# GLU and long convolution on one core: a list schedule with other transfer constants and ranks, the first tile split over two DMA queues, one weight cast moved to VectorE

## The chip, the cores and the metric

The kernel runs on one core of one Trainium2 chip. The metric is the device time of one execution in microseconds (us); the median of three runs counts. TensorE (PE) multiplies; VectorE (DVE) and ScalarE (ACT) do element-wise work; GpSimd (POOL) and SyncE (SP) mostly issue transfers; PEld is TensorE's weight load, which lies beside its matmuls.

## What is computed

For tokens x of 2048 x 512 the kernel computes a gated mix of a state-space convolution and a bilinear GLU (cut to what matters, with x = A_u):

```python
g = sigmoid((x * gate_w).sum(-1, keepdims=True))
K = 2.0 * einsum("dn,dnl->dl", C, exp(A * dt * l)).real      # 512 channels, 128 states, 2048 taps
a = irfft(rfft(x, 4096) * rfft(K, 4096))[:2048] + x * D_skip  # a causal convolution per channel
b = ((x @ w_gate) * (x @ w_up)) @ w_down                      # 512 -> 1792 -> 512
out = g * a + (1 - g) * b
```

All inputs are float32.

## The kernel before

**The GLU.** The 1792 hidden channels are 14 tiles of 128, in four groups (0-2, 3-5, 6-9, 10-13); the tokens are four columns of 512, and the 512 model channels four tiles kt of 128. To keep float32 accuracy, each operand is split in a high and a low part: ACT casts the high part to the matmul's type, and DVE subtracts it from the original, which leaves the low part. A product is then three matmuls of 128 x 128 by 128 x 512 (high-low, low-high, high-high; the first ones of the kernel in the other order, so that those that need low parts come last). The names: `xs` holds both parts of a token tile, `whi` and `wlo` the gate and up weights, `pg` and `pu` the two PSUM banks of gate and up. From them ACT copies `h` out of `pg` (which also frees that bank), DVE multiplies it by `pu`, ACT casts `hh`, DVE makes `hl`, and these multiply the down weights `dhi`, `dlo` into the bank `y`. `product` (line 668), `hidden` (684) and `down` (711) hold these steps; `evacuate` (722) takes `y` out.

**The convolution.** DVE, ACT and POOL make tables of powers, `x` and `v` (`x_table`, line 1099, and `v_table`, 1123); from these TensorE makes the kernel's taps (`k_block`, 1164) and then transforms of 128 points (`k_first`, `m_product`, `m_inverse`, `m_last`), whose PSUM tiles are all called `k`. `u_part` (819) loads the tokens a second time and computes the scores of the gate: DVE's `y<-in,w3s` in the trace.

**What sets the order.** Every step is a task with an engine, an estimated duration, the tiles that it reads and writes, a rank and, for a transfer, a cost `dma`. `Work.plan` (355) is a list scheduler: it always takes the task that can start first by its own model (ties by rank), and the instructions are issued in that order on each engine by `InOrder` (line 124, which is therefore the line of nearly all instructions in the profile). The model of a transfer is: `SENT` us after its issue it enters one of two modelled queues, which share the rate by `WEIGHT`; it needs `dma` by `DMA_RATE`; and `LANDED` us later its readers may start. `FETCH` and `BEYOND` are terms for the loading of TensorE's instructions, `ROOM` says how much an ordinary task may delay an urgent one, and `EASE` is a table that gives tasks of a given engine, tiles and duration a slack in us, a rank or a later place. The schedule is fixed when the kernel is built; on the chip each engine goes through its list and waits on semaphores.

**The start.** `first_loads` (577) issues the first token tile (`xsrc(0)`, 256 KB, tile `y`) on SP and the first 256 columns of the first weights (128 KB, tile `ev`: a strip of gate and a strip of up columns) on ACT's queue, then the other kt by SP. `warm` runs six plain matmuls on a zeroed tile while these transfers are under way. `first_split` (626) makes `whi` and `wlo` of each kt, and `split` (541) the parts of `xs`. Ahead of its first cast ACT has an ACT_TABLE_LOAD, which the compiler inserts.

The functions touched:

Of the kernel before, what the change touches and what calls it, by code (L numbers as in the profile page):

```python
# [10 lines left out]
F32 = mybir.dt.float32  # L11
# [7 lines left out]
P = 128  # L19
# [185 lines left out]
class Work:  # L205
# [15 lines left out]
    BLOCK, FIRST, LEAD, FETCH = 256, 193, 64, 5.0  # L221
    TABLE = 1.3
    ROOM = {"dve": 0.6, "act": 0.4}
    BEYOND = 60
# [3 lines left out]
        "act:k/e:0.4": (3, 0, 0),  # L228
        "act:pb/x:0.31": (0.0, 0, -60),
# [4 lines left out]
        "dve:in/whi/wlo:0.69": (0.0, 1, 0),  # L234
        "dve:k/in:0.42": (3, 0, 0),
        "dve:k/ri:0.7": (0.0, 1, 0),
        "pe:kt/k/ri/e:2.13": (0.0, 0, -200),
        "pool:ts:0.95": (2, 0, 0),
# [4 lines left out]
    SENT = {"sp": 1.15, "act": 1.15, "pool": 1.98}  # L243
    LANDED = {"sp": 1.79, "act": 1.79, "pool": 1.5}
# [205 lines left out]
def gated_mix_kernel(  # L450
# [126 lines left out]
    def first_loads():  # L577
# [6 lines left out]
        wsrc = wts[0][:, : 2 * D].rearrange("p (k d) -> p k d", k=2)  # L584
# [41 lines left out]
    def first_split(kt):  # L626

        hi, lo, t, k = *ws[0], raws["w0"], ("k", kt)
        cut = lambda x: x.rearrange("p (c d) -> p c d", c=2)[:, :, P * kt : P * kt + P]
        src = lambda: t.t[:, :, P * kt : P * kt + P]  # L630
        add("act", 0.38, lambda: act.copy(cut(hi.t), src()), r=[(t, k)], w=[(hi, k)], rank=0)
# [16 lines left out]
    def tokens(gi, ci, kt):  # L648

        x = xs[kt] = new("glu", "xs", [P, 2, D], F32R, 5)  # L650
        if gi:
            add("sp", 0.42, lambda: sp.dma_start(x.t.bitcast(F32), xs_d[ci, kt]), r=[(m_xs, (ci, kt))], w=[x], dma=422, rank=0)
# [921 lines left out]
```

## Time and profile before

| | |
|---|---|
| three runs | 581.23, 581.37, 582.0; median 581.37 us |
| the profiled execution | 581.93 us, of which the span 580.1 |
| TensorE busy | 573.5 us, 99% |
| DVE, ACT, POOL busy | 510.9, 401.6, 113.5 us (88%, 69%, 20%) |
| chain of waits that ended last | PE 97%, a DMA 1%, ACT 1%, DVE 1% |
| data moved | 136.28 MB, 235 GB/s on average |

Busy shares alone say that TensorE is the bound. What is not TensorE's is found in three views: the waits of PE (how long it stood, and for whom), the windows (busy time of PE in stretches cut at its stalls), and the timeline around each stall. A row of the timeline has its start, its length, engine, line, operation with output and inputs, shape, and in brackets the idle time before it with what ended it.

### The profile page before, as it was taken

What the parts mean: (1) busy time and instruction counts of PE and PEld (TensorE: products, weight loads), DVE (VectorE), ACT (ScalarE), POOL (GpSimd) and SP (SyncE); (2) the same over time, 40 slices, a digit from 0 to 9 for tenths busy, and PEclk for the clock granted to TensorE, in tenths of its full rate; (3) what the DMA queues carried; (4) which work ended last, traced back from release to release, by engine and by line L of the source; (5) the groups of instructions that cost most, each with busy time, mean ns of one, the idle gap of its engine ahead of it and who ended that gap; (6) DMA issues with size and microseconds to landing.
All of it is one profiled execution on the core that took longest, in us unless ns stands there. A gap on an engine that the chain in (4) does not pass through costs nothing.

```text
span 580.1 us, 14843 instructions
## 1 busy us (share of the span) xinstructions
PE 573.5 (99%) x5998; PEld 433.8 (75%) x5998; DVE 510.9 (88%) x812; ACT 401.6 (69%) x891; POOL 113.5 (20%) x159
## 2 busy tenths in 40 slices
PE   9999999999999999999999999999999999999997
PEld 6777776888886877788677878876868786776775
DVE  6999999999998999999999999997999996347655
ACT  5459888898588589967896775799877544343351
POOL 0003222311111150321132401102333103111011
PEclk9999999999999999999999999999999999999999
DMA  8999959998655797998779757978989439798986
GB/s 284 403 354 358 395 216 354 269 231 232 140 173 128 281 228 173 261 216 273 201 226 250 188 135 238 213 198 206 292 147 292 72 134 289 246 293 222 291 166 128
DMA packets 71687, 136.28 MB, mean 235 GB/s; under 512 B 6852, under 2 KB 35780, under 8 KB 69188
## 3 DMA queue, kind: packets, MB, share of 16 engines
q1 hardware_dynamic: 47668, 87.10, 43.7%
q0 software_dynamic: 23392, 47.98, 39.6%
q8 instruction: 47, 0.77, 0.6%
q10 hardware_dynamic: 560, 0.26, 0.2%
q14 instruction: 20, 0.16, 0.1%
HBM read 80.27 MB, written 55.05 MB: 233 GB/s over the span
## 4 chain that ended last, share of the span: by engine, by line
PE 97%; DMA 1%; ACT 1%; DVE 1%; issue 0%; DVEq 0%; ACTq 0%
PE pg L124 27%; PE y L124 27%; PE pu L124 27%; PE k L124 16%; DMA y<-in_xT 1%; ACT h L124 0%; DVE y L124 0%; ACT acc L124 0%; ACT xs L124 0%; DVE hl L124 0%; DVE dlo L124 0%; DVE kt L124 0%; DVEq L1568 0%; ACT whi L124 0%; DVE h L124 0%
## 5 line engine op out<-in xcount | busy, mean ns | idle before, releaser
L124 PE MATMUL pg<-xs,whi 128*128 128x512 f32 x448 | 138.9, 391 | 0.4 <-ACT whi L124 0.4
L124 PE MATMUL pu<-xs,whi 128*128 128x512 f32 x448 | 138.2, 390 | 0.0
L124 PEld LDWEIGHTS pg<-xs,whi 128*128 128x128 f32 x448 | 84.3, 188 | 17.7 <-ACT whi L124 0.6
L124 PEld LDWEIGHTS pu<-xs,whi 128*128 128x128 f32 x448 | 84.1, 188 | 17.0
L124 PE MATMUL y<-dhi,hl 128*128 128x512 f32 x224 | 90.2, 403 | 0.7 <-DVE hl L124 0.6
L124 PE MATMUL pg<-xs,wlo 128*128 128x512 f32 x224 | 89.9, 401 | 0.8 <-ACT h L124 0.7
L124 PE MATMUL pu<-xs,wlo 128*128 128x512 f32 x224 | 89.3, 399 | 0.0
L124 PE MATMUL y<-dlo,hh 128*128 128x512 f32 x224 | 87.6, 391 | 0.0
L124 PE MATMUL y<-dhi,hh 128*128 128x512 f32 x224 | 87.1, 389 | 0.0
L124 POOL DMA_DIRECT2D out<-acc x44 | 38.5, 930 | 171.6 <-ACT acc L124 171.0
L124 ACT COPY ev<-k 128x512 f32<-128x512 f32 x112 | 59.3, 597 | 15.8 <-PE k L124 13.3
L124 ACT CAST hh<-h 128x512 fp32r<-128x512 f32 x56 | 34.7, 620 | 41.7 <-DVE h L124 41.3
L124 DVE TENSOR_TENSOR h<-pu,h 128x512 f32<-128x512 f32 x56 | 38.6, 689 | 26.3 <-PE pu L124 23.9
L124 ACT ACTIVATE acc<-y,ngate 128x512 f32<-128x512 f32 x62 | 42.0, 689 | 24.3 <-PE y L124 23.2
L124 PEld LDWEIGHTS pg<-xs,wlo 128*128 128x128 f32 x224 | 42.1, 188 | 21.5 <-issue 10.1
L124 PEld LDWEIGHTS y<-dhi,hl 128*128 128x128 f32 x224 | 42.0, 187 | 21.6 <-issue 8.3
L124 ACT COPY h<-pg 128x512 f32<-128x512 f32 x56 | 33.0, 590 | 32.4 <-PE pg L124 28.6
L124 PEld LDWEIGHTS pu<-xs,wlo 128*128 128x128 f32 x224 | 42.0, 188 | 16.7 <-issue 7.0
L124 PEld LDWEIGHTS y<-dhi,hh 128*128 128x128 f32 x224 | 42.1, 188 | 9.0
L124 PEld LDWEIGHTS y<-dlo,hh 128*128 128x128 f32 x224 | 42.1, 188 | 8.1 <-issue 0.3
L124 DVE TENSOR_TENSOR hl<-h,hh 128x512 fp32r<-128x512 f32 x56 | 38.4, 686 | 3.6 <-ACT hh L124 3.1
L124 DVE TENSOR_TENSOR v<-m,v 128x896 f32<-128x896 f32 x32 | 34.0, 1084 | 0.2
(130 smaller groups left out, 959.1 us busy)
## 6 DMA issues: line engine op xcount, KB each, us to landing
xs<-xs_d SPq DMA_DIRECT2D x36, 512.0 KB, 5.8
out<-acc POOLq DMA_DIRECT2D x44, 256.0 KB, 6.4
raw<-in_wts SPq DMA_DIRECT2D x33, 256.0 KB, 4.9
xs_d<-xs SPq DMA_DIRECT2D x16, 512.0 KB, 6.8
su_d<-ev POOLq DMA_DIRECT2D x32, 256.0 KB, 6.1
y_d<-ts SPq DMA_DIRECT2D x28, 256.0 KB, 6.1
in<-su_d POOLq DMA_DIRECT2D x12, 512.0 KB, 8.0
sk_d<-ev SPq DMA_DIRECT2D x6, 1024.0 KB, 3.9
```

Source lines behind the costliest of these rows:

```text
L124: got = getattr(self.engine, name)(*args, **kw)
```

## The change

It has five parts.

1. Constants of the planner: `WEIGHT` of the second queue 1.58 to 1.24, `FETCH` 5 to 4, `ROOM` of DVE 0.6 to 1.0, `BEYOND` 60 to 90, `SENT` and `LANDED` of all queues, the `dma` cost of some fifteen transfers, the slack of `k_block` 1 to 2, and a new `EASE` table. None of it adds or removes an instruction; it gives another order.
2. The first token tile is brought by two transfers of 64 rows each, one on SP's queue and one on ACT's, ahead of the weights' there.
3. The gate and up columns of weight tile 0 are laid out on the host so that each kt's 256 columns lie together; `first_loads`, `first_split` and `product` follow.
4. For kt = 0 the high part of the weights is made by DVE (`tensor_copy`) and not by ACT.
5. `product` gets the number f in place of the weights, to choose the base of its columns.

```diff
-    WEIGHT = 1.0, 1.58
+    WEIGHT = 1.0, 1.24
...
-    BLOCK, FIRST, LEAD, FETCH = 256, 193, 64, 5.0
+    BLOCK, FIRST, LEAD, FETCH = 256, 193, 64, 4.0
     TABLE = 1.3
-    ROOM = {"dve": 0.6, "act": 0.4}
-    BEYOND = 60
+    ROOM = {"dve": 1.0, "act": 0.4}
+    BEYOND = 90
...
-        "act:ts/xs:0.62": (0.0, 2, 0),
-        "dve:ev/y:0.6": (3, 0, 0),
+        "dve:ev/y:1.23": (0.0, 0, 200),
...
-    SENT = {"sp": 1.15, "act": 1.15, "pool": 1.98}
-    LANDED = {"sp": 1.79, "act": 1.79, "pool": 1.5}
+    SENT = {"sp": 1.35, "act": 1.35, "pool": 1.86}
+    LANDED = {"sp": 1.56, "act": 1.56, "pool": 1.62}
...
+        flat = w0.t.rearrange("p k d -> p (k d)")
         for kt in range(KT):
 
-            t, k, ks = xt[kt // 2], kt % 2, slice(P * kt, P * kt + P)
-            add("sp", 0.42, lambda t=t, k=k, kt=kt: sp.dma_start(t.t[:, k], xsrc(kt)), w=[(t, k)], dma=256, rank=-1)
+            t, k, ks = xt[kt // 2], kt % 2, slice(2 * P * kt, 2 * P * kt + 2 * P)
             e, q = ("sp", sp) if kt else ("act", act)
-            add(e, 0.42, lambda q=q, ks=ks: q.dma_start(w0.t[:, :, ks], wsrc[:, :, ks]), w=[(w0, ("k", kt))], dma=128, rank=-1)
+            cuts = (slice(0, P // 2), slice(P // 2, P)) if kt == 0 else (slice(0, P),)
+            for n, cut in enumerate(cuts):
+                ex, qx = ("act", act) if n else ("sp", sp)
+                add(
+                    ex, 0.42, lambda t=t, k=k, kt=kt, cut=cut, qx=qx: qx.dma_start(t.t[cut, k], xsrc(kt)[cut]),
+                    w=[(t, (k, n)) if len(cuts) > 1 else (t, k)], dma=256 // len(cuts), rank=-1,
+                )
+            add(e, 0.42, lambda q=q, ks=ks: q.dma_start(flat[:, ks], wts[0][:, ks]), w=[(w0, ("k", kt))], dma=128, rank=-1)
...
-        add("act", 0.38, lambda: act.copy(cut(hi.t), src()), r=[(t, k)], w=[(hi, k)], rank=0)
+        if kt:
+            add("act", 0.38, lambda: act.copy(cut(hi.t), src()), r=[(t, k)], w=[(hi, k)], rank=0)
+        else:
+            add("dve", 0.35, lambda: dve.tensor_copy(cut(hi.t), src()), r=[(t, k)], w=[(hi, k)], rank=0)
...
-        base = which * D + kt * P
+        base = which * D + kt * P if f else 2 * kt * P + which * P
...
-        add("pe", 2.05, kgen, r=[x, v], w=[pk], rank=0, hold=[kt], count=256, slack=1.0)
+        add("pe", 2.05, kgen, r=[x, v], w=[pk], rank=0, hold=[kt], count=256, slack=2.0)
...
+    wts[0, :, : 2 * D] = wts[0, :, : 2 * D].reshape(P, 2, KT, P).transpose(0, 2, 1, 3).reshape(P, 2 * D)
```

What that does to the engines' lists is shown at three places. A row is line, operation, output and inputs, and in brackets the semaphores that it waits for (DMAHW are those of transfers on SP's and ACT's queues; two transfers of different numbers are two waits).

**The start, on ACT.** Before, from its first transfer to its third cast:

```order
L124 DMA ev<-in_wts 128x2x128
L124 DMA small<-in_rows 128x4
L124 ACT_TABLE_LOAD
L124 CAST xs<-y 128x512 [waits DMAHW1_49]
L124 CAST whi<-ev 128x2x128 [waits DMAHW0_49]
L124 CAST xs<-y 128x512 [waits DMAHW2_49]
```

Now:

```order
L124 DMA y<-in_xT 64x512
L124 DMA ev<-in_wts 128x256
L124 DMA small<-in_rows 128x4
L124 ACT_TABLE_LOAD [waits DMAHW1_49]
L124 CAST xs<-y 128x512 [waits DMAHW0_49]
L124 CAST xs<-y 128x512 [waits DMAHW2_49]
L124 CAST whi<-ev 128x256 [waits DMAHW4_49]
```

A transfer of half the token tile (64 rows) has come first in the list; the cast of `whi` for kt = 0 has gone; the first cast reads a tile that two transfers write, and one of its two waits, DMAHW1, which is SP's half, stands at the table load's row.

**The start, on DVE.** Before, from its first subtraction:

```order
L124 TENSOR_TENSOR xs<-y,xs 128x512 [waits DMAHW1_49,Activation_49]
L124 TENSOR_TENSOR wlo<-ev,whi 128x2x128 [waits DMAHW0_49,Activation_49]
L124 TENSOR_TENSOR xs<-y,xs 128x512 [waits DMAHW2_49,Activation_49]
L124 TENSOR_TENSOR wlo<-ev,whi 128x2x128 [waits DMAHW4_49,Activation_49]
L124 TENSOR_SCALAR small<-small 128x4 [waits DMAHW3_49]
```

Now:

```order
L124 TENSOR_TENSOR xs<-y,xs 128x512 [waits DMAHW1_49,DMAHW0_49,Activation_49]
L124 CAST whi<-ev 128x256 [waits DMAHW3_49]
L124 TENSOR_TENSOR wlo<-ev,whi 128x256 [waits DVE_49]
L124 TENSOR_TENSOR xs<-y,xs 128x512 [waits DMAHW2_49,Activation_49]
L124 TENSOR_TENSOR wlo<-ev,whi 128x256 [waits DMAHW4_49,Activation_49]
L124 TENSOR_SCALAR small<-small 128x4 [waits DMAHW5_49]
```

A cast of the weights' 256 columns has come in behind the first subtraction, which waits for both halves.

**Some 25 us in, on DVE and PE** (`hl_358` and `hl_376` are the same tile in the two kernels, the low part of the third hidden tile; `y_323` and its like are scores). DVE before:

```order
L124 TENSOR_TENSOR h_313<-pu_309,h_313 128x512 [waits PE_49,Activation_49]
L124 SCALAR_TENSOR_TENSOR y_341,gate_83<-in_181,w3s_162 128x512
L124 TENSOR_TENSOR dlo_349<-kt_153,dhi_329 128x512 [waits DMAHW4_49,Activation_49]
L124 SCALAR_TENSOR_TENSOR y_354,gate_83<-in_181,w3s_162 128x512 [waits DVE_49]
L124 TENSOR_TENSOR hl_358<-h_313,hh_343 128x512 [waits Activation_49]
L124 SCALAR_TENSOR_TENSOR y_360,gate_83<-in_181,w3s_162 128x512 [waits DVE_49]
L124 TENSOR_TENSOR xs_336<-ts_237,xs_336 128x512 [waits DMAHW5_49]
```

DVE now:

```order
L124 TENSOR_TENSOR h_313<-pu_309,h_313 128x512 [waits PE_49,Activation_49]
L124 SCALAR_TENSOR_TENSOR y_346,gate_83<-in_182,w3s_167 128x512 [waits DVE_49]
L124 TENSOR_TENSOR xs_336<-ts_238,xs_336 128x512 [waits DMAHW6_49,Activation_49]
L124 SCALAR_TENSOR_TENSOR y_356,gate_83<-in_182,w3s_167 128x512 [waits DVE_49]
L124 TENSOR_TENSOR dlo_364<-kt_158,dhi_354 128x512 [waits DMAHW5_49,Activation_49]
L124 TENSOR_SCALAR ngate_84<-gate_83 128x4 [waits Activation_49]
L124 TENSOR_SCALAR gate_83<-gate_83 128x4 [waits DVE_49]
L124 TENSOR_TENSOR hl_376<-h_313,hh_348 128x512
```

The low part of a token tile of the next column, dlo and the two steps on the gates now stand ahead of `hl`. PE before, from the second pair of down products to the third:

```order
L124 MATMUL y_345<-dhi_275,hl_302 128x512
L124 MATMUL y_345<-dlo_283,hh_295 128x512
L124 MATMUL y_345<-dhi_275,hh_295 128x512
L124 MATMUL y_331<-dhi_329,hl_358 128x512 [waits DVE_49]
L124 MATMUL y_331<-dlo_349,hh_343 128x512 [waits Activation_49]
```

PE now:

```order
L124 MATMUL y_342<-dlo_315,hh_290 128x512
L124 MATMUL y_342<-dhi_304,hh_290 128x512
L124 MATMUL pg_358<-xs_336,wlo_148 128x512 [waits Activation_49]
L124 MATMUL pg_358<-xs_336,whi_144 128x512 [waits DVE_49]
L124 MATMUL pg_358<-xs_336,whi_144 128x512
L124 MATMUL pu_368<-xs_336,wlo_148 128x512
L124 MATMUL pu_368<-xs_336,whi_144 128x512 x2
L124 MATMUL y_330<-dhi_354,hl_376 128x512 [waits DVE_49,Activation_49]
```

Six matmuls of the next column's `pg` and `pu` now stand between.

**Some 420 us in, on ACT** (`ts` are output tiles of the convolution, mixed with the gate; `h_5475` and `h_5426` are the same copy of a `pg` in the two kernels, which frees its bank). Before, from the last mixes:

```order
L124 ACTIVATE ts_5276<-ts_5276,gate_83 128x128 x5
L124 CAST dhi_5433<-raw_5303 128x512 [waits DMAHW3_49]
L124 CAST hh_5439<-h_5322 128x512 [waits DVE_49]
L124 COPY x_5445<-pb_4184 128x64 [waits PE_49]
L124 CAST dhi_5447<-raw_5309 128x512 [waits DMAHW4_49]
L124 COPY kt_5455<-k_5324 128x8x2x16
L124 COPY v_752<-ri_5155 128x32x4
L124 COPY v_752<-ri_5155 128x32x7
L124 COPY v_752<-ri_5155 128x32x4
L124 COPY v_752<-ri_5155 128x32x7
L124 COPY h_5475<-pg_5423 128x512 [waits DVE_49,PE_49,Activation_49]
```

Now:

```order
L124 COPY v_881<-ri_5124 128x32x7
L124 COPY x_5399<-pb_4104 128x64
L124 COPY h_5426<-pg_5379 128x512 [waits DVE_49,PE_49]
L124 CAST dhi_5429<-raw_5280 128x512 [waits DMAHW3_49]
L124 COPY ts_5436<-k_5408 128x2x256 [waits DMAHW2_49,PE_49]
L124 CAST dhi_5443<-raw_5306 128x512 [waits DMAHW4_49]
L124 COPY ts_5447<-k_5418 128x2x256 [waits PE_49]
L124 ACTIVATE v_881<-v_881 128x32x16 [waits DVE_49,Activation_49]
L124 ACTIVATE sq_5456<-v_881 128x512 [waits Activation_49]
L124 CAST hh_5475<-h_5426 128x512 [waits DVE_49]
L124 ACTIVATE ts_5436<-ts_5436,gate_83 128x128 x2
L124 ACTIVATE ts_5436<-ts_5436,gate_83 128x128 [waits DVE_49]
```

Before, the copy of `h` stands behind all sixteen mixes, two casts and four copies; now behind the four copies and ahead of the casts and of the first eight mixes. On PE a transform's sixteen matmuls (`k` from `w4_t`) now stand between the last `pg` of that copy and its `pu`, where none stood.

More of the change, by code (lines that the diff above doesn't have):

```diff
@@ L218 @@
     OVERLAP = {"act": 0.09, "dve": 0.08}
-    BLOCK, FIRST, LEAD, FETCH = 256, 193, 64, 5.0
+    BLOCK, FIRST, LEAD, FETCH = 256, 193, 64, 4.0
     TABLE = 1.3
-    ROOM = {"dve": 0.6, "act": 0.4}
-    BEYOND = 60
+    ROOM = {"dve": 1.0, "act": 0.4}
+    BEYOND = 90
     BEHIND = 1.3
     EASE = {
-        "act:k/e:0.4": (3, 0, 0),
-        "act:pb/x:0.31": (0.0, 0, -60),
+        "act:k/e:0.6": (3, 0, 0),
+        "act:k/ev:0.6": (0.0, 2, 0),
+        "act:kt/dhi:0.62": (3, 0, 0),
         "act:raw/whi:0.62": (0.0, 0, -60),
         "act:t/rt:0.77": (0.0, 0, -200),
-        "act:ts/xs:0.62": (0.0, 2, 0),
-        "dve:ev/y:0.6": (3, 0, 0),
-        "dve:in/whi/wlo:0.69": (0.0, 1, 0),
+        "dve:ev/y:1.23": (0.0, 0, 200),
         "dve:k/in:0.42": (3, 0, 0),
-        "dve:k/ri:0.7": (0.0, 1, 0),
-        "pe:kt/k/ri/e:2.13": (0.0, 0, -200),
-        "pool:ts:0.95": (2, 0, 0),
+        "dve:x/ps/ri/su/di/m:1.09": (0.0, 0, 60),
         "sp:w3s/w2s/v:1.3": (0.0, 1, 0),
@@ L655, in tokens @@
         split(x, x, (0, 1), ("x", gi, ci, kt))
[L656 removed]
+        add("sp", 0.42, lambda: sp.dma_start(xs_d[ci, kt], x.t.bitcast(F32)), r=[x], w=[(m_xs, (ci, kt))], dma=443, rank=2, after=16.0 + kt if ci == 0 else 0.0)
     def ahead(ci):
@@ L666, in gated_mix_kernel, with product @@
     THREE = ((1, 0), (0, 1), (0, 0))
-    def product(pg, which, w, x, kt, after, first):
-        base = which * D + kt * P
+    def product(pg, f, which, x, kt, after, first):
+        w = ws[f]
+        base = which * D + kt * P if f else 2 * kt * P + which * P
         part = ("k", kt) if first else which
@@ L694, in hidden @@
         for which, kt in pairs:
-            product(pg[which], which, ws[f], x[kt], kt, after, not steps[1:] and f == 0)
+            product(pg[which], f, which, x[kt], kt, after, not steps[1:] and f == 0)
         h = new("glu", "h", [P, D])
@@ L735, in evacuate @@
         elif gi == 0:
-            add("sp", 0.42, lambda: sp.dma_start(ov[:, t, :], acc.t), r=[acc], w=[(m_out, t)], dma=134)
+            add("sp", 0.42, lambda: sp.dma_start(ov[:, t, :], acc.t), r=[acc], w=[(m_out, t)], dma=196)
         else:
@@ L739, in evacuate @@
                 "pool", 0.95, lambda: pool_q.dma_start(ov[:, t, :], acc.t, accum_op=ALU.add),
-                r=[acc, (m_out, t)], dma=431, rows=[t],
+                r=[acc, (m_out, t)], dma=442, rows=[t],
             )
@@ L821, in u_part @@
         rs = slice(4 * t, 4 * t + 4)
-        add("sp", 0.42, lambda: sp.dma_start(ut.t, uv[:, rs, :]), w=[ut], dma=929, after=6.0 + (U_STEP + 1.0) * t)
+        add("sp", 0.42, lambda: sp.dma_start(ut.t, uv[:, rs, :]), w=[ut], dma=840, after=6.0 + (U_STEP + 1.0) * t)
         def score_of(j):
@@ L880, in first @@
                     ),
[L881 removed]
+                    r=[st], w=[(m_su, (q, n0))], dma=234,
                 )
@@ L1236, in k_first @@
                     ),
-                    r=[st], w=[(m_sk, (q, m)) for m in range(n0, n0 + n, 8)], dma=41 * n,
+                    r=[st], w=[(m_sk, (q, m)) for m in range(n0, n0 + n, 8)], dma=50 * n,
                 )
@@ L1249, in gated_mix_kernel, with w_load @@
     m_w4 = work.memory()
-    def w_load(tag, shape, src, kb=327):
+    def w_load(tag, shape, src, kb=394):
         t = new("mid", tag, shape, bufs=2)
@@ L1274, in m_load @@
                 ),
-                r=[(m, (q, n0)) for n0 in range(0, 32, 8 if w else 4)], w=[(t, (T, w))], dma=655 if w else 585,
+                r=[(m, (q, n0)) for n0 in range(0, 32, 8 if w else 4)], w=[(t, (T, w))], dma=574 if w else 544,
             )
@@ L1458, in m_last @@
                 lambda rs=rs, flat=flat: pool_q.dma_start(ov[:, rs[0] : rs[-1] + 1, cs], flat(), accum_op=ALU.add),
-                r=[*parts, *((m_out, r) for r in rs)], dma=119 * len(rs), rows=rs,
+                r=[*parts, *((m_out, r) for r in rs)], dma=129 * len(rs), rows=rs,
             )
@@ L1544 @@
         "in_xT": host(u[rows.T.reshape(L)].T),
-        "in_wts": host(
-            np.concatenate(
-                [by_tile(i["B_w_gate"]), by_tile(i["B_w_up"]), i["B_w_down"].reshape(NF, P, D)], axis=2
-            )
-        ),
+        "in_wts": host(wts),
         "in_prm": host(
```

18 lines of the change are left out of this document (8 added, 10 removed).

## The prediction

> **What bounds the kernel now.** First the page: the span, the busy times, and the chain of work that ended last.
>
> ```profile
> span 580.1 us, 14843 instructions
> PE 573.5 (99%) x5998; PEld 433.8 (75%) x5998; DVE 510.9 (88%) x812; ACT 401.6 (69%) x891; POOL 113.5 (20%) x159
> PE 97%; DMA 1%; ACT 1%; DVE 1%; issue 0%; DVEq 0%; ACTq 0%
> ```
>
> TensorE is busy for 99% of the span. The order of both kernels holds the same matmuls and the same number of switches between the GLU and the convolution, so the change can only move what TensorE does not fill. The waits of PE name it, in total, times and longest:
>
> ```profile
> PE k L124 <- DVE acc L124: 1.1, 1, 1.1
> PE pg L124 <- ACT h L124: 0.7, 1, 0.7
> PE y L124 <- DVE hl L124: 0.6, 1, 0.6
> PE pg L124 <- ACT whi L124: 0.4, 1, 0.4
> ```
>
> And the windows of PE, cut at the stalls, show where (length, busy time and matmuls, granted clock, DMA share, GB/s):
>
> ```profile
> 0.00:5.62 5.62, 4.21 (x7) 1.00 0.64 177
> 25.33:26.27 0.94, 0.38 (x2) 1.00 1.02 405
> 26.27:100.00 73.73, 73.62 (x404) 1.00 0.93 340
> 100.00:420.00 320.00, 320.00 (x3723) 1.00 0.84 216
> 420.00:422.00 2.00, 1.33 (x6) 1.00 0.77 234
> 422.00:576.40 154.40, 154.27 (x1780) 1.00 0.80 207
> 576.40:580.10 3.70, 0.00 (x0) 0.99 0.64 196
> ```
>
> Three things can move: the 5.62 us before the first real matmul, two stalls (at 25.3 and 420.6), and 0.11 + 0.13 us in the long windows. The 3.70 us after the last matmul have the same order of work in both kernels and stay. So the most that stalls can give back is below 2 us, 0.3%; a measurement of this kernel can tell about 0.2%, 1.16 us, from no change. The start decides the sign.
>
> **The start, before.** The longest first piece of the chain of waits, then ACT, DVE and PE in time (start, length, what ended the idle time):
>
> ```profile
> 0.74 3.88 DMA y<-in_xT
> ```
>
> ```profile
> 1.75 1.28 ACT L124 ACT_TABLE_LOAD   x1 [1.75 <-issue]
> 4.64 0.62 ACT L124 CAST xs<-y 128x512 fp32r<-128x512 f32 x1 [1.60 <-DMA y<-in_xT]
> 5.17 0.40 ACT L124 CAST whi<-ev 128x256 fp32r<-128x256 f32 x1
> ```
>
> ```profile
> 0.84 0.17 DVE L124 MEMSET acc<- 128x128 f32 x1 [0.84 <-PEq L1563]
> ...
> 5.29 0.69 DVE L124 TENSOR_TENSOR xs<-y,xs 128x512 fp32r<-128x512 f32 x1 [4.13 <-ACT xs L124]
> 5.90 0.42 DVE L124 TENSOR_TENSOR wlo<-ev,whi 128x256 fp32r<-128x256 f32 x1
> ```
>
> ```profile
> 1.06 4.21 PE L124 MATMUL k<-acc 128*128 128x512 f32 x6 [1.06 <-DVE acc L124]
> 5.62 1.17 PE L124 MATMUL pg<-xs,whi 128*128 128x512 f32 x2 [0.35 <-ACT whi L124]
> 6.63 0.40 PE L124 MATMUL pg<-xs,wlo 128*128 128x512 f32 x1
> 6.86 0.62 PE L124 MATMUL pu<-xs,whi 128*128 128x512 f32 x2
> ```
>
> The first tile lands at 0.74 + 3.88 = 4.62. ACT casts its high part from 4.64, then the weights' from 5.17; DVE makes the low parts from 5.29 and 5.90; the first real matmul starts at 5.62, the third at 6.63, and from there they come every 0.23 us (6.86 - 6.63). The table load of 1.28 us, at 1.75, costs nothing: it lies in the shadow of the transfer, and ACT then sits idle for 1.60 us.
>
> **The first tile by two queues.** The cast now needs two landings, one per queue. An instruction row has the other wait: in the order of the changed kernel it is the table load, inserted ahead of the cast, that holds the wait for SP's half, while the cast itself keeps the wait for ACT's half. If the load waits in its row, its cover is gone: it starts when SP's half is in, and the cast 1.28 us after that. When does the half land? At latest when the whole tile did, 4.62. For the other end, the data flow in the DMA view of the first 8 us (40 slices of 0.2 us):
>
> ```profile
> GB/s 0 0 0 0 0 0 0 0 10 92 154 133 205 259 218 205 189 202 205 251 306 348 391 331 326 372 331 394 374 399 333 399 341 343 364 325 384 382 330 333
> y<-in_xT SPq DMA_DIRECT2D x4, 256.0 KB, 4.8
> ev<-in_wts ACTq DMA_DIRECT2D x1, 128.0 KB, 4.3
> ```
>
> Bytes move from 1.6 on, so at most 3.0 us of the tile's 3.88 are its own flow, and half of its bytes would save 1.5 at the very best (landing 3.1). But the nearest row, a 128 KB transfer on ACT's queue beside a 256 KB one on SP's, took 4.3 us from issue to landing, longer than the 3.88 of the 256 KB tile: a transfer of half the size is no faster there. I take 0.2 us earlier, 4.42.
>
> The Trainium skill, "DMA: Bandwidth & Descriptors", Rules for kernel authors, speaks against this part: two transfers to disjoint partition halves are not worth it, since both spread over the same 16 DMA engines and serialize. By it the second of the two halves would land at 4.62, and the sum below would be up to 0.2 us higher; the 4.3 us row agrees with it as far as it goes.
>
> So ACT's cast starts at 4.42 + 0.02 + 1.28 = 5.72, 1.08 later than 4.64. ACT's first weight transfer goes out one issue later than before; it is needed only two steps later, on DVE.
>
> **The weights' high part by VectorE.** On DVE it stands behind the low part of x: so after 5.72 come 0.65 (5.29 - 4.64, from ACT's start to DVE's), 0.61 (5.90 - 5.29, one DVE step), the copy itself, and 0.05 until PE (5.62 against the end of ACT's at 5.57). No row of before shows such a copy on DVE; it lies between a memset of 128 columns, 0.17, and the subtraction of the same 256 columns, 0.42, and I take 0.30, the middle, since ACT's copy of the tile took 0.40. The first matmul then starts at 5.72 + 0.65 + 0.61 + 0.30 + 0.05 = 7.33. The low part of the weights follows on DVE, until about 7.7. The third matmul of the kernel starts two steps after the first: 7.79 if they run at 0.23 us, 8.34 if they take the 1.01 us they took before (6.63 - 5.62). Against 6.63 that is +1.16 or +1.71. I take +1.45 for the start; DVE's and ACT's following pieces each take less than the six matmuls (1.38 us) that they feed, and all landed by then, so nothing more is lost behind it. The ends: +0.2 with the half at 3.1 and the copy at 0.17, +2.0 with the half at 4.62, the copy at 0.42 and the slow pace.
>
> The re-laid columns of the first weights change the shape of a transfer from two strips per row to one; PE reads the same 128 columns, at no cost on its side.
>
> **The stall at 25.3.** DVE's and PE's rows:
>
> ```profile
> 23.10 0.69 DVE L124 TENSOR_TENSOR h<-pu,h 128x512 f32<-128x512 f32 x1 [0.26 <-PE pu L124]
> 23.71 0.68 DVE L124 SCALAR_TENSOR_TENSOR y<-in,w3s 128x512 f32<-128x512 f32 x1
> ...
> 24.32 0.69 DVE L124 TENSOR_TENSOR dlo<-kt,dhi 128x512 fp32r<-128x512 f32 x1
> ...
> 25.53 0.69 DVE L124 TENSOR_TENSOR hl<-h,hh 128x512 fp32r<-128x512 f32 x1
> ```
>
> ```profile
> 25.33 0.39 PE L124 MATMUL y<-dhi,hh 128*128 128x512 f32 x1
> 26.27 0.50 PE L124 MATMUL y<-dhi,hl 128*128 128x512 f32 x1 [0.56 <-DVE hl L124]
> ```
>
> From start to start PE lost 0.94 - 0.23 = 0.71 us because hl came 2.43 us behind h on DVE, behind a score, dlo and a score. In the new order 18 matmuls stand between the last pu and that y, where 12 stood, which gives hl 6 x 0.23 = 1.38 us more; but on DVE four steps of 0.61 (a score, the low part of x, a score, dlo) stand between h and hl where three stood, and two small ones on the gates, which I take at 0.15 each, near the 0.17 of the memset; so hl ends about 0.9 us later. 0.71 - 1.38 + 0.9 = 0.2 us stay; with 0.4 for the upper end I take -0.3 here.
>
> **The stall at 420.6.** ACT's and PE's rows:
>
> ```profile
> 419.77 1.46 ACT L124 COPY v<-ri 128x128 f32<-128x128 f32 x4
> 421.04 0.62 ACT L124 COPY h<-pg 128x512 f32<-128x512 f32 x1
> ```
>
> ```profile
> 420.42 0.61 PE L124 MATMUL pu<-xs,whi 128*128 128x512 f32 x2
> 421.71 0.50 PE L124 MATMUL pg<-xs,wlo 128*128 128x512 f32 x1 [0.67 <-ACT h L124]
> ```
>
> PE's second matmul started near 420.65, the next at 421.71: 1.06 - 0.23 = 0.83 us lost, since the copy that frees the bank stood behind sixteen mixes, two casts and four copies. In the new order that copy stands ahead of mixes and casts, and on PE a transform's sixteen matmuls come between this pg and its pu, so this stall goes. The next copy of h now stands behind eight mixes, one of which waits for DVE; if that copy is late, some comes back. I take -0.7 (from 0 to -0.83).
>
> **New stalls.** Most of the 812 and 891 instructions of DVE and ACT stand in a new order, with other due times for transfers. What that costs no trace shows; the order of before, made by the same planner, left two stalls of 0.7 to 0.8, so zero to two such ones bound it, and I take +0.3, the middle being high for an order fitted to landings.
>
> **Sum.** +1.45 - 0.3 - 0.7 + 0.3 = +0.75 us. The profiled execution took 581.93 (580.1 of span and 1.83 around it), which gives 582.7; it lies 0.56 above the median of the three runs, 581.37, so the forecast of the median is 582.1, slower by 0.13%. Ends: start +0.2 and both stalls gone, -1.2; start +2.0, two new stalls and none gone, +3.5.
>
> **Rivals.**
>
> *The clock is lost at the start (slower).* The rows of the warming matmuls and of others with the same 512 columns:
>
> ```profile
> L124 PE MATMUL k<-in,w_t 64*32 64x512 f32 x96 | 5.8, 595 | 0.0
> L124 PE MATMUL k<-acc 128*128 128x512 f32 x4 | 3.8, 1101 | 1.1 <-DVE acc L124 1.1
> ```
>
> The granted clock reads 1.00 throughout, yet the first took 1101 ns and not 595: half speed until about 6.6. Before, PE's idle time between the warming and the real work was 0.35 us; after, it would be 7.33 - 5.27 = 2.06. If the full speed has to be earned again from there, matmuls run at 0.23 x 1101/595 = 0.42; eight of them lose 1.5 us, and the time is 583.6. It decides if the third real matmul and those behind it still stand 0.4 apart. For it: in this trace the speed came only after the gap. Against it: full speed may come sooner than the warming ends in most executions. 18%.
>
> The Trainium skill, "TensorE: Matmul & The Clock Gate", Part 1, has this as a free-running window of about 3.4 us that must be busy before the clock goes to full; by it the loss depends on where the window falls in an execution. Only the two groups above bear on that here.
>
> *The load is not held (no change).* If the table load runs at 1.75 as before, since ACT runs it ahead of its wait, the cast starts at 4.44, the first matmul at 6.05, the third at 6.5 to 7.1: start +0.15, sum -0.55, 580.8. For it: nothing but that the load needs no data. Against it: an engine's row waits where it stands. 17%, two thirds of it within 0.2%.
>
> *The new order clears PE's way (faster).* Both stalls go whole (-1.54), no new one comes, and the two halves land near 3.1 (start +0.2): -1.34, 580.0. Its place is the two stalls; it decides when the start costs under 0.4 us. 8%.
>
> *New stalls (slower).* Two of 0.8 us at new places and the rest as in the forecast: start +1.45, stalls +1.6 - 1.0: +2.05, 583.4. 7%.
>
> **How the numbers follow.** The forecast has 50%, from 581.0 to 583.4, between the start's two paces and the stalls' bounds; a third of it lies above 582.53, where slower than 0.2% begins (17%), the rest within 0.2% (33%). With the clock (18%) and new stalls (7%), slower is 42%. Within 0.2%: 33 + 11 = 44%. Faster: 8 + 6 = 14%. The range leaves out half of the faster cases and the worst tail of the slow ones: 580.5 to 584.2.
>
> **What would show it.** Right: the table load starting at 4.3 to 4.7 and ending just ahead of the first cast; whi on DVE behind the low part of x; the first pg near 7.3; no wait of PE at 420 and a small one near 27. Wrong: the table load at 1.7; the first pg before 6.3; matmuls 0.4 apart up to 10 us; a wait of over 0.5 us elsewhere.

## The result: 1% slower, and the profile after

The changed kernel takes 587.89 us, median of four runs (587.79 to 589.28), against 581.68 for the kernel before in the same comparison: a ratio of 1.0099, interval 1.0077 to 1.0121. The forecast, 582.1 in 580.5 to 584.2, was too low by 5.8 us. The profiled execution of the changed kernel took 587.79, 5.86 more than that of before, and its parts can be set beside the prediction's.

From the page, the engines' busy time and the chain that ended last:

```profile
PE 575.4 (98%) x5998; PEld 435.0 (74%) x5998; DVE 511.7 (87%) x813; ACT 399.2 (68%) x890; POOL 113.6 (19%) x159
PE 86%; DMA 5%; issue 4%; POOL 1%; ACT 1%; DVE 1%; SPq 0%; DVEq 0%; POOLq 0%; ACTq 0%
```

TensorE still has the same 5998 instructions, but the chain now leaves it: DMA 5%, issue 4% and POOL 1%, which were 1%, 0% and nothing. ("Issue" is time in which an engine waits for nothing that the profile shows.) The waits of PE say where:

```profile
PE pg L124 <- DVE whi L124: 3.1, 1, 3.1
PE k L124 <- issue: 1.5, 2, 0.8
PE k L124 <- DVE acc L124: 1.1, 1, 1.1
PE y L124 <- DVE hl L124: 0.6, 1, 0.6
PE k L124 <- DMA in<-sk_d: 0.4, 1, 0.4
PE pg L124 <- ACT h L124: 0.2, 1, 0.2
```

**The start.** ACT, DVE and PE in time:

```profile
4.92 1.28 ACT L124 ACT_TABLE_LOAD   x1 [4.92 <-DMA y<-in_xT]
6.21 1.14 ACT L124 CAST xs<-y 128x512 fp32r<-128x512 f32 x2
```

```profile
6.87 0.69 DVE L124 TENSOR_TENSOR xs<-y,xs 128x512 fp32r<-128x512 f32 x1 [5.71 <-ACT xs L124]
7.48 0.28 DVE L124 CAST whi<-ev 128x256 fp32r<-128x256 f32 x1
```

```profile
1.06 3.76 PE L124 MATMUL k<-acc 128*128 128x512 f32 x6 [1.06 <-DVE acc L124]
7.91 1.19 PE L124 MATMUL pg<-xs,whi 128*128 128x512 f32 x2 [3.09 <-DVE whi L124]
8.89 0.63 PE L124 MATMUL pg<-xs,wlo 128*128 128x512 f32 x1
9.32 1.05 PE L124 MATMUL pu<-xs,whi 128*128 128x512 f32 x2
...
15.11 0.50 PE L124 MATMUL pg<-xs,wlo 128*128 128x512 f32 x1
```

The table load, which ran at 1.75 before, starts at 4.92 with the landing of the first tile's half, and the first cast right behind it. The first real matmul comes at 7.91 (5.62 before), the third at 8.89 (6.63). And they then run slowly: from 8.89 to 9.32 is 0.43, where it was 0.23. The windows of PE show the clock with it (length, busy time and matmuls, granted clock):

```profile
7.91:10.82 2.91, 2.91 (x7) 0.50 0.98 383
10.82:15.11 4.29, 4.29 (x18) 0.97 0.95 338
```

For these 2.9 us TensorE had half its clock. The matmul that opens the second hidden tile is the row at 15.11 above; before, it stood at 11.81, in the row below. So 3.30 us are lost by then, 2.29 until the first matmul and 1.0 behind it, where the clock is low.

```profile
11.81 0.50 PE L124 MATMUL pg<-xs,wlo 128*128 128x512 f32 x1
```

**The rest.** From there to the last matmul before had 564.2 us and the changed kernel 566.9, 2.7 more. PE's rows near 131, 418, 334 and 466; the last fence is the kernel before:

```profile
129.86 1.98 PE L124 MATMUL k<-v,x 128*32 128x64 f32 x124
132.53 0.31 PE L124 MATMUL k<-v,x 128*32 128x64 f32 x4 [0.69 <-issue]
...
416.20 1.88 PE L124 MATMUL k<-v,x 128*32 128x64 f32 x119
418.86 0.35 PE L124 MATMUL k<-v,x 128*32 128x64 f32 x9 [0.79 <-issue]
```

```profile
334.26 1.60 PE L124 MATMUL k<-in,w2s 32*32 32x512 f32 x32 [0.39 <-DMA in<-sk_d]
...
465.76 2.13 PE L124 MATMUL k<-in,w2s 32*32 32x512 f32 x32
```

```profile
457.94 1.99 PE L124 MATMUL k<-v,x 128*32 128x64 f32 x128
...
462.13 1.14 PE L124 MATMUL k<-in,w2s 32*32 32x512 f32 x32
```

The long runs of 128 small matmuls that make the kernel's taps break off for 0.69 and 0.79 us, 4 and 9 matmuls ahead of their end, and the profile shows nothing that they wait for; such a run went through before. In the window from 129 to 133 the DMA view has a transfer of the queue called instruction:

```profile
q8 instruction: 1, 0.02, 1.5%
```

so code that came late fits. But that queue brings 47 packets in the whole run, one in 12 us, and one of them in such a window says little: the cause is not shown. The pass at 466 took 2.13 us for 32 matmuls, and such a pass took 1.14 before; this profile doesn't say why, but in e6 and e17 below the same pass is broken by a wait for `kt` from DVE. The pass at 334 first waits for a transfer, the 0.4 of `in<-sk_d` above, and then takes 1.60. The stall at 420.6 is gone as forecast; the one at 25 stands at 31 now and costs 0.78 where it cost 0.71; one of 0.33 from start to start is new near 341. Start to start, the two breaks cost 1.8 (0.69 + 0.79 of it idle time), the pass at 466 1.0, the wait at 334 with its pass 0.9, the stall at 341 0.3 and the one at 31 0.1 more, less 0.83 for the stall that went: 3.3. The measured 2.7 is 0.6 less, which no single row shows.

### The profile page after: what moved, and what is told of

It is laid out like the page before. It is cut to its first block, busy times and chain, and to the rows that moved or that the text cites. A ratio compares the mean times of both kernels' runs of the same rounds, so it can differ in the third digit from the quotient of the medians.

```text
span 586.0 us, 14853 instructions
## 1 busy us (share of the span) xinstructions
PE 575.4 (98%) x5998; PEld 435.0 (74%) x5998; DVE 511.7 (87%) x813; ACT 399.2 (68%) x890; POOL 113.6 (19%) x159
## 4 chain that ended last, share of the span: by engine, by line
PE 86%; DMA 5%; issue 4%; POOL 1%; ACT 1%; DVE 1%; SPq 0%; DVEq 0%; POOLq 0%; ACTq 0%
PE y L124 24%; PE pg L124 23%; PE pu L124 23%; PE k L124 15%; DMA ts<-in_xT 1%; DMA kt<-in_wts 1%; DMA out<-acc 1%; POOL in L124 1%; DMA y<-in_xT 1%; DMA sk_d<-ev 1%; ACT ev L124 1%; POOL out L124 1%; SPq L124 0%; DVE y L124 0%; ACT h L124 0%
## 5 line engine op out<-in xcount | busy, mean ns | idle before, releaser
L124 PEld LDWEIGHTS k<-v,x 128*32 128x32 f32 x2048 | 29.5, 110 | 7.4 <-issue 6.4
```

What stands on the lines that cost most here:

```text
L124: got = getattr(self.engine, name)(*args, **kw)
```

## The experiments

Times are ratios to the kernel before in the same comparison, with their intervals; single rows are from each kernel's profiled execution. For the profiled executions two numbers are given: the start of the matmul that opens the second hidden tile (11.81 before, 15.11 changed), which is the start's cost, and the time from it to the start of the last matmul (564.2 and 566.9), the rest's.

### The start: what it costs, and why

`e12_after_again` is the changed kernel once more, without an edit.

> The changed kernel once more, beside the others on one chip. All theories: 0.8 to 1.2% slower than before; first real matmul near 7.9, matmuls 0.43 apart to about 10.5, two waits for issue near 131 and 418.

1.0092 (1.0073 to 1.0111): the loss is there again. Opening matmul 16.71, rest 566.3; of the two breaks only the one near 131 came (0.65).

`e1_early_table` gives ACT an operation that needs no transfer, so that the table load has somewhere else to go:

```diff
...
+        def small_in():
+            act.dma_start(small[:, 0], rows[1].rearrange("(p c) -> p c", c=KT))
+            act.copy(early, half_pi)
...
```

> The changed kernel with one ACT copy of 128x1 behind ACT's third transfer, so that the table load no longer stands behind the first tile's landing. Theory (load held by the first landing, and the long gap of PE costs its clock): load near 2.5, first cast at 4.9, first real matmul near 6.6 instead of 7.9, 1.3 us less, and up to 1.4 more if PE's clock is then full sooner: 585.2 to 586.6 beside 587.9. Rival (the halves' late landing or DVE's cast sets the start): first real matmul stays past 7.5, time within 0.5 us of 587.9.

```profile
2.45 1.28 ACT L124 ACT_TABLE_LOAD   x1 [2.45 <-issue]
3.74 0.19 ACT L124 COPY early<-fixed 128x1 f32<-128x1 f32 x1
4.40 0.62 ACT L124 CAST xs<-y 128x512 fp32r<-128x512 f32 x1 [0.47 <-DMA y<-in_xT]
```

ACT's rows: the load is back in the shadow, the cast at 4.40, the first real matmul at 6.10 (7.91). 1.0054 (1.0038 to 1.007): some 0.4% of the 0.95% come back, more than the 1.28 us of the load. The two breaks grew, to 1.5 and 1.7 from start to start.

`e17_act_cast` leaves the load where the change put it and gives the first weights' cast back to ACT:

```diff
-        if kt:
+        if True:
             add("act", 0.38, lambda: act.copy(cut(hi.t), src()), r=[(t, k)], w=[(hi, k)], rank=0)
```

> The changed kernel with the first weights' cast back on ACT, and the table load left behind the first landing; PE's list unchanged. Theory (load and cast each cost, and the later the start, the longer the slow clock): load at 4.9, first cast at 6.2, first real matmul near 7.2 instead of 7.9, 0.7 to 1.5 us less than the changed kernel: 0.65 to 0.85% above before. Rival (the load alone costs): first real matmul earlier but the time unchanged, 0.92 to 0.99%.

The first matmul came at 7.01 and the opening one at 14.41, 0.7 earlier, yet the time stayed: 1.0093 (1.0063 to 1.0122). The rival's number, but not its reason: the profile lost 1.0 at the pass near 332 (0.56 of it a wait for `in<-sk_d`), 1.13 for h near 340 and 1.5 at the pass near 465 instead (start to start), and shows no break of the long runs. `e11_early_act` has both repairs, with PE's list untouched.

> The changed kernel with the early ACT copy, and the first weights' cast back on ACT; PE's list unchanged. Theory: load out of the way, first cast near 4.4, cast of the weights at 4.95, first real matmul near 5.4 to 5.7 where it was 6.1 with DVE's cast: 0.3 to 0.7 us less at the start, clock full sooner; the code waits take part of it back: 0.3 to 0.5% above before. Rival (DVE's cast costs nothing, since the low parts bind): first real matmul earlier but the third one not, the same time as with the early copy alone, 0.55% above before.

1.0029 (1.0015 to 1.0044): together they bring back two thirds of the loss. In the profile the first matmul is at 6.09, the opening one at 12.80, and the rest is 564.4, that of before. So only 2.3 us of the 4.7 between the two profiles lie at the start: the rest was healed too, which no theory had said. The waits near 334 and 341 are gone in it, and so is the break near 130; a break of 0.7 near 413 and the late pass (1.99 us at 461) stay.

`e4_one_tile` brings the first tile by one transfer again:

```diff
-            cuts = (slice(0, P // 2), slice(P // 2, P)) if kt == 0 else (slice(0, P),)
+            cuts = (slice(0, P // 2), slice(P // 2, P)) if kt < 0 else (slice(0, P),)
```

> The changed kernel with the first tile by one transfer on SP's queue; the same list of PE. Theory (the second landing puts the load behind the first): load at 1.75, first cast near 4.65, first real matmul near 6.3, 1.6 us less, and 0.7 to 1.4 more by the clock: 584.9 to 586.3. Rival (the weights' cast on DVE is the start's cost): first real matmul later than 7, less than 0.9 us gained: 587.0 to 587.9.

The load ran at 1.66, the cast at 4.68, and the first matmul at 5.35, earlier than expected, since the weights' cast stood ahead of x on DVE here (4.88 and 5.33). But 1.0071 (1.0046 to 1.0096). In the profiled execution, the slowest of the six (589.74), the rest took 571.0, with breaks of 1.8 and 2.0 from start to start in the runs at 129 and 417, 0.8 at the pass near 332 and 1.1 for h near 340; a wait of 1.2 for h lies ahead of it.

`e14_start_in_place` puts the changed start into the kernel before, inside its tasks, so that PE keeps the order of before. (The first cast on DVE lies ahead of the low part of x there.)

```diff
...
+            def tile_in(t=t, k=k, kt=kt, cuts=cuts):
+                for n, cut in enumerate(cuts):
+                    (act if n else sp).dma_start(t.t[cut, k], xsrc(kt)[cut])
...
```

> The kernel before with its order kept on PE, and the changed start put into it: the first tile's halves on two queues, the weights re-laid, their first cast on DVE (here ahead of the low part of x). Theory (load behind the landing, then slow clock): load at 4.9, first cast at 6.2, first real matmul near 6.9, up to 1.4 us of slow matmuls, no wait for issue: 1.3 to 3 us, 0.2 to 0.5% above before. Rival (the loss is the new order's): within 0.2% of before.

1.0016 (1.0000 to 1.0033). Load at 4.90, first cast 6.19, first matmul 6.86, slow matmuls behind it (0.43 apart past 10 us), opening matmul 14.81, rest 564.7. The profiled execution, 585.49, was the slowest of its ten runs, which begin at 582.98. Its mean granted clock was 0.995 and that of the nine others 1.000, so what the clock takes varies by execution.

`e15_halves_in_place` does the same with the early copy and all casts on ACT.

> The kernel before with its order kept, the first tile's halves on two queues, the early ACT copy, all casts on ACT. Theory: load out of the way, first cast at 4.4 to 4.9 where it was 4.64, first real matmul 5.3 to 5.8: within 0.2% of before; the halves are worth 0.3 us at most. Rival (halves land earlier as such, and are what the change wanted): 0.5 us or more below before.

1.0009 (0.9996 to 1.0022): first cast 4.65, first matmul 5.62, both as before the change. The two halves are worth nothing here: SP's landed later than the whole tile had, as the DMA view of the changed kernel already showed (KB each, us to landing):

```profile
y<-in_xT ACTq DMA_DIRECT2D x1, 128.0 KB, 3.3
y<-in_xT SPq DMA_DIRECT2D x1, 128.0 KB, 4.1
```

One half is 0.6 faster than the 3.88 us of the whole tile, the other 0.2 slower, and both are needed. The Trainium skill, "DMA: Bandwidth & Descriptors", Rules for kernel authors, says of two such halves not to bother; the trace agrees.

**The clock.** `e2_long_warm` and `e16_warm_four` keep PE busy in the gap, with seven and four more warming matmuls of 512 columns (two PE instructions each). The edit of the second:

```diff
-            for n in (4, 4, 1):
+            for n in (4,) * 6 + (1,):
```

> The changed kernel with seven more warming matmuls, so that PE's gap before the first real matmul closes; nothing else moves. Theory (the gap of 3.1 us drops the clock): first real matmul still at 7.9, but matmuls 0.23 apart from there, 1.4 us less: 586.5. Rival (the first real matmuls are slow for a reason other than the gap): still 0.43 apart to 10.8, time 587.9.

> The changed kernel with four more warming matmuls, sized to end near the first real one. Theory (PE's gap costs its clock): PE's gap under 0.5 us, first real matmul at 7.9 to 8.3, matmuls 0.23 apart from there, 1 to 1.4 us less than the changed kernel: 0.7 to 0.75% above before. Rival (no clock lost by the gap): 0.43 apart as before, no gain: 0.9 to 1%.

PE's rows of the second:

```profile
1.05 8.54 PE L124 MATMUL k<-acc 128*128 128x512 f32 x14 [1.05 <-DVE acc L124]
9.35 0.71 PE L124 MATMUL pg<-xs,whi 128*128 128x512 f32 x2
9.90 0.39 PE L124 MATMUL pg<-xs,wlo 128*128 128x512 f32 x1
10.13 0.62 PE L124 MATMUL pu<-xs,whi 128*128 128x512 f32 x2
```

With no gap the real matmuls are 0.23 apart at once (10.13 - 9.90): without it the clock is full when they begin. But the warming matmuls ran at half pace until about 7 us themselves (0.85 apart, then 0.43), and the real ones began 1.4 us later than in the changed kernel, so that the opening matmul was at 15.07, as there; with seven more it was at 17.43. Times: 1.0069 (1.0043 to 1.0094) with four, 1.0115 (1.0073 to 1.0158) with seven. Neither number measures the clock alone. With either the breaks near 131 and 418 are gone or under 0.3, while PE waits 2.6 (seven) and 1.8 us (four) for `in<-sk_d` near 335: PE's few added instructions shift all that follow. In the profile with seven the table load started at 3.65, since SP's half landed that early; in the others that hold the load behind it, it started at 4.74 to 5.15. So a landing differs by over 1 us between executions.

### The planner's constants

`e6_planner_only` is the change without its start.

```diff
-            cuts = (slice(0, P // 2), slice(P // 2, P)) if kt == 0 else (slice(0, P),)
...
+            add("sp", 0.42, lambda t=t, k=k, kt=kt: sp.dma_start(t.t[:, k], xsrc(kt)), w=[(t, k)], dma=256, rank=-1)
```

> The changed kernel's constants, ranks and order with the start of before (one transfer for the first tile, weights in two strips, all casts on ACT); PE's list is that of the changed kernel. Theory (start and code waits each cost, and code waits take back what the start gives): first real matmul near 5.6, 3.7 us gained at the start, the two waits for issue grow to some 2 us each and take 2 back: 0.6% above before. Rival (the start is the whole loss): at most 0.3% above before.

1.0071 (1.0049 to 1.0093). The start was that of before (first matmul 5.69, opening one 11.77), and still 0.7% were lost, all of it in a rest of 568.9: breaks of 0.9 and 1.4 near 129 and 416, 1.2 at the pass near 465, 0.7 at the one near 331 and 1.0 for h near 338.

`e5_start_only` is the opposite: the changed start with the constants of before, from which the planner makes an order of its own.

> The changed start (two halves, weights re-laid, first cast on DVE) with the constants and ranks of before; the planner makes an order of its own from these. Theory (start and code waits): load behind the landing, first real matmul near 7.9, slow matmuls behind it, no wait for issue over 0.3: 3 to 4 us, 0.5 to 0.7% above before. Rival (the new constants are the whole loss): within 0.2% of before.

1.0248 (1.0224 to 1.0272), outside all expectations. A change of a few tasks at the start alone gave an order some 14 us worse.

`e3_fetch` takes back `FETCH` and `BEYOND`. Only `FETCH` moves PE's list: the two runs after it, with `FETCH` alone, have the same one.

```diff
-    BLOCK, FIRST, LEAD, FETCH = 256, 193, 64, 4.0
+    BLOCK, FIRST, LEAD, FETCH = 256, 193, 64, 5.0
...
-    BEYOND = 90
+    BEYOND = 60
```

> The changed kernel with FETCH 5 and BEYOND 60, as before; all other constants, ranks and the start stay. Theory (the planner's terms for the loading of PE's instructions let long runs of k matmuls stand where their code is late): the two waits of PE for nothing but issue (0.69 near 131, 0.79 near 418) go, 1.5 to 1.8 us less: 586.1 to 586.4. Rival (they belong to any order of this kind): one or two such waits of 0.7 or more at other places, time within 0.5 of 587.9.

1.0113 (1.0087 to 1.0139). The breaks are gone, but the rest took 569.1, with 0.9 for h near 339, 2.2 for kt at 344 and 1.25 for h at 471. With the good start, `e13_fetch_early_act`:

> The changed kernel with FETCH 5, the early ACT copy and all casts on ACT. Theory of code waits: none for issue over 0.3 us; 3 us less than FETCH 5 alone had, some 0.6 to 0.8% above before, since the order that FETCH 5 gives waits for kt, h and pg instead. Rival (those waits came from the late start): within 0.3% of before.

1.0010 (0.9995 to 1.0026), rest 564.4: level with before, on a list of PE that lost 1.1% in the run before, and with breaks of 0.96 and 0.91. And with the start of before, `e18_planner_fetch`:

> The changed kernel's constants but FETCH 5, with the start of before: PE's list is that of FETCH 5. Theory (code waits, once the start is early): no wait of PE for issue over 1 us, 2 to 3.5 us less than the same start with FETCH 4: 0.1 to 0.35% above before. Rival (what the start of before lost on the new order came from elsewhere): 0.6 to 0.75% above before, as with FETCH 4.

1.0083 (1.0061 to 1.0105), rest 569.4. The theory of code waits fell here: `e13` and `e18` have one list of PE and both a first matmul before 5.8, yet lie 0.7% apart, and it isn't breaks that part them. What the slow one has is a wait for h. PE's, ACT's, POOL's and SP's rows of it:

```profile
337.98 0.78 PE L124 MATMUL pg<-xs,wlo 128*128 128x512 f32 x1 [2.18 <-ACT h L124]
```

```profile
330.70 0.86 ACT L124 ACTIVATE rt<-t,fixed 128x672 f32<-128x672 f32 x1 [0.68 <-DVE t L124]
336.76 0.69 ACT L124 ACTIVATE acc<-y,ngate 128x512 f32<-128x512 f32 x1 [5.21 <-DMA out<-acc]
337.35 0.58 ACT L124 COPY h<-pg 128x512 f32<-128x512 f32 x1
```

```profile
305.86 1.58 POOL L124 DMA_DIRECT2D out<-ts  x1 [2.67 <-DVE v L124]
318.49 1.56 POOL L124 DMA_DIRECT2D out<-ts  x1 [11.06 <-ACT acc L124]
```

```profile
307.29 2.58 SPq L124 DMA_DIRECT2D xs<-xs_d  x4
```

Read backwards: PE waits 2.18 us for h, h stands on ACT behind an evacuation that waits 5.21 for a buffer `acc`, this is freed by a transfer on POOL's queue, and that queue has been late since its transfer of the first `ts` tile at 305.86. The view of that tile says how late (us from issue to landing):

```profile
DMA to landing us min/median/max: 12.3/12.3/12.3
```

The same transfer lands in 6.8 us before. Over the profiles it has two kinds of landing: 6 to 8 us where it set out at least 2 us ahead of SP's loads of `xs` (before, e1, e11, e13, e14, e15), 12 to 13 where it set out 0.4 to 1.4 ahead (e2, e3, e4, e6, e16, e17, e18, and the changed kernel with 12.4). In e12, 0.95 ahead, the view gives no landing, but POOL's next transfer starts 13.2 us later, as in the second kind. PE's wait for h near 340 is 0.3 to 2.3 from start to start in all of the second kind but e2, and absent from the first. On the list of the changed kernel the second kind also has PE's wait for `in<-sk_d`, near 334 in the changed kernel: 0.3 to 2.6 us of idle time (the 2.6 is e2), and none in e1 and e11. That transfer too is on POOL's queue behind the `ts` tiles. It set out at 329.07 in the changed kernel and at 321.16 in e11, 7.9 us apart, where PE's pass that reads it stood only 3.7 apart (334.26 and 330.52).

### The race of two transfers

Three experiments try to hold back the loads of `xs`, with small transfers put ahead of them:

```diff
...
+                if (gi, ci, kt) == (2, 2, 1):
+                    for n in range(4):
+                        sp.dma_start(pad[:, n], rows[1].rearrange("(p c) -> p c", c=KT))
                 sp.dma_start(x.t.bitcast(F32), xs_d[ci, kt])
...
```

> The changed kernel with four small transfers put ahead of SP's loads of xs near 310 us, so that these start some 2 us later; all else as it is. Theory of the lost race (POOL's transfer of the first ts tile at 309 lands in 12 us and not 7, since the loads of xs set out 1.3 us behind it; all POOL transfers behind it come late, ACT waits for one of them, and h with it): that transfer lands in under 9 us, no wait of PE for h near 341, but only 0.1 to 0.9 us less in all, since the start and the code waits stay: 0.8 to 0.95% above before. Rival (the landing is slow for another reason): it takes 12 us again, time unchanged.

> The start of before on the constants of the change but FETCH 5, with the loads of xs near 308 us held back by four small transfers. Theory of the lost race: the first ts tile lands in under 9 us, the wait of 2.2 us for h near 335 and the slow clock behind it go, 2 to 4.5 us less: 0.1 to 0.5% above before where it was 0.83%. Rival (landing slow for another reason): again 12 us, 0.8%.

> The start of before on all constants of the change, with the loads of xs near 308 us held back by four small transfers. Theory of the lost race: the first ts tile lands in under 9 us, no wait for h near 338, 0.8 to 2.5 us less than the 0.71% above before that it had: 0.3 to 0.6%; what is left are the code waits near 129 and 416. Rival: again 12 us, 0.7%.

1.0114 (1.0096 to 1.0133), 1.0094 (1.0075 to 1.0113) and 1.0075 (1.0053 to 1.0097): nothing. But the loads had not been held back (1.0 to 1.2 behind, landings of 12.6 to 13.2): they wait for their buffers, and the small ones went out in that wait. So these three say nothing on the race. `e22_xs_apart` is `e18_planner_fetch` with six small ones between the first load and the other three:

```diff
...
+                if (gi, ci, kt) == (2, 2, 2):
+                    for n in range(6):
...
```

> The start of before on the constants of the change but FETCH 5, with six small transfers between the first load of xs near 307 us and the three that follow it, which so start some 2.5 us later (ahead of the first they had not held it back, since it waits for its buffer). Theory of the lost race: the first ts tile lands in 9 us or less, the wait of 2.2 us for h near 335 shrinks to under 0.7, 1.5 to 4 us less than the 0.83 to 0.94% above before that it had. Rival (the landing is slow for a reason other than these loads): 12 us again, 0.8 to 0.95%.

SP's rows, POOL's and ACT's, and the landing of both `ts` tiles in that stretch (the first is the 8.4):

```profile
307.41 0.32 SPq L124 DMA_DIRECT2D xs<-xs_d  x1
307.77 3.98 SPq L124 DMA_DIRECT2D pad<-in_rows  x6
311.84 2.39 SPq L124 DMA_DIRECT2D xs<-xs_d  x3
```

```profile
305.73 1.58 POOL L124 DMA_DIRECT2D out<-ts  x1 [2.65 <-DVE v L124]
314.42 1.56 POOL L124 DMA_DIRECT2D out<-ts  x1 [7.11 <-ACT ev L124]
```

```profile
333.86 0.69 ACT L124 ACTIVATE acc<-y,ngate 128x512 f32<-128x512 f32 x1 [2.18 <-DMA out<-acc]
```

```profile
DMA to landing us min/median/max: 8.4/8.9/9.4
```

The three loads set out at 311.84, the `ts` tile lands in 8.4 us, the next POOL transfer starts at 314.4 and not 318.5, ACT waits 2.18 for `acc` and not 5.21, and PE has no wait for h. 1.0036 (1.0024 to 1.0049), from 1.0083: 0.47% of the time, 2.7 us, by six transfers of 2 KB. On this list the race is the cause of that much. Another wait grew meanwhile: the one for kt near 341 is 1.4 us, where e18 has 0.3.

None of the kernels beats the one before; `e15_halves_in_place` and `e13_fetch_early_act` are level with it.

## Why the prediction was wrong

**Right.** The table load took SP's wait and left its shadow: "it starts when SP's half is in", at 4.92. The sum for what follows was close: 0.66 from ACT's start to DVE's (0.65), 0.61, a cast of 0.28 (0.30). The half landed 0.5 later than taken, at about 4.9 and past the "at latest" of 4.62: that bound had been taken from one transfer on one queue. The start's +1.45 measured +2.26 at the third matmul, past its upper end of +2.0: the slow pace's +1.71, and 0.55 mostly by the landing. By the opening matmul it was +3.3. The stall at 420.6 went.

**Wrong on the chance: the clock.** It was a rival at 18%, +1.5 us. In the changed kernel's profile it cost 1.0 until the opening matmul. Matmuls 0.43 apart (0.42 taken) stand behind the gap in the profiles of e1, e3, e12, e14 and e17 too, but in two ways. In e1, e3 and e17 the six warming matmuls take 4.21 us, as before, and the view shows no fall: by the pace, the clock was not yet full when the gap came. Here and in e12 they took 3.76 and 3.65, so the clock was up before 4.8, as the prediction had held against the rival, and the gap of 3.09 (2.06 taken) lost it again. In e14 (4.15) it fell too, at 8.43, behind a gap of 1.65. The windows around the fall and the rise:

```profile
7.60:7.90 0.30, 0.00 (x0) 0.54 1.22 331
10.90:11.20 0.30, 0.30 (x2) 0.77 1.06 396
```

With half the clock as 0.50, these put the fall at 7.62 and the rise at 11.04. The Trainium skill, "TensorE: Matmul & The Clock Gate", Part 1, has the clock fall after an idle window of about 3.4 us and rise after a busy one, at a free-running phase. The spread between executions agrees with the phase, and the time at half clock with the length of the window (3.42 here, 3.42 in e14, 6.82 in e12). On the length of the gap the traces differ, since the gap of 3.09 here and one of 2.18 in e18 (below) were enough.

**Wrong on the size: the 25 us stall.** 0.71 was to shrink by 0.3; it stayed (31.03 against 29.79 + 0.23 for the second of two: 0.78). The steps between h and hl on DVE took what the sum gave them (3.30 from start to start, 3.35 in the sum), but h, at 26.90, no longer started when pu was done: in the new order DVE comes to it late, without idle time. The sum moved hl against h and left h where it was.

**Wrong at the step "new stalls".** This term is the largest miss of the sum. It took +0.3, with two stalls of 0.8 as the far end, from what the order of before had left. The changed kernel has some 4.0 us of them (two breaks, a late pass, a wait for `in<-sk_d` with its pass, a wait for h). Beside the forecast of +0.75 the profile has: start +3.3 (1.45 taken), stall at 25 us +0.1 (-0.3), stall at 420 -0.8 (-0.7), new stalls +4.0 (+0.3), and -0.7 that no row shows, in all the measured 5.9. The failed thought is that a planner's order has stalls of a size that its last order shows. The runs show in its place that the order is good only for the timing in which it was found: the same list of PE takes 564.4 or 568.9 us behind the start (e11, e6), a list with `FETCH` 5 564.4, 567.3, 569.1 or 569.4 (e13, e22, e3, e18), and the constants of before with the changed start lose 2.5% (e5). For one of these losses the mechanism is shown, the race of POOL's first `ts` transfer with the loads of `xs`: set out 1.4 us ahead it is lost (e18), 2.25 ahead it is won (e1). The changed kernel lost that race too (12.4 us). By the chain of waits that cost it 1.2 us of PE's time, 0.9 at 334 and 0.3 at 341, but no run here wins the race in it with all else left alone.

The sum's lower end was also added a little wrong: a start of +0.2 with both stalls gone is -1.34, as the rival says, and not -1.2. Nothing hangs on it.

**What stays open.** What breaks the runs of `k<-v,x` is not settled: the breaks are 0 to 2 us in kernels with one list of PE, come at the same place (4 and 9 matmuls ahead of the end in e1 and e4 as well), go with eight added PE instructions (e16), grow with one ACT copy (e1), and `FETCH` 5 does not prevent them (e13). Nor is it shown what puts POOL's transfer some 0.9 us or more earlier against the loads in e1, e11 and e13; all three have the early copy, so their gain is partly the won race, and the load and the cast can't be priced apart from it. And how much of the start's loss is the clock differs by execution: in place on the order of before it cost 1 us in the median (e14) and 3.6 in the profile.

## What to carry to other kernels

An instruction that the compiler inserts ahead of another can take over one of its waits: look in the order for the waits of a table load before splitting a transfer that an ACT operation reads, and give ACT an early operation that needs no data. A start that leaves TensorE idle for 3 us can cost its clock besides, here 1.0 us. And a schedule fitted by constants holds for one timing: after any shift, even one that should only gain, look for the transfer whose landing has doubled, and at the queue behind it.

## What the runs showed of the hardware

A transfer of a 512 KB tile on POOL's queue, which is added to what lies at its target, lands in 12 to 13 us when it is set out 0.4 to 1.4 us ahead of four 512 KB loads on SP's; with 2 us or more between them, or with three of the four held back, in 6 to 8.4. The granted clock falls in the middle of a kernel too: in e18, behind the wait of 2.18 us near 336, it is 0.50 in the windows of PE:

```profile
336.00:338.00 2.00, 0.02 (x1) 1.00 1.09 198
338.00:341.00 3.00, 3.00 (x7) 0.50 0.77 109
```

so a stall of 2 us there costs some 1.3 more (seven matmuls in 3.0 us where thirteen fit at 0.23). The clock does not need a gap of full length to fall: in the 3.4 us ahead of its fall PE had stood for 2.8 us in the changed kernel, 2.2 in e18 and 1.9 in e14. A gap of 1.42 in e11 and one of 1.20 in e4 did not bring it down.
